# One-token attention block on one core: groups of one kv head over all batches instead of single (batch, head) pairs

## The chip, the core and the metric

The kernel runs on one core of a Trainium2 chip. A core has a matrix engine (TensorE, PE in the profile, with its weight loads as PEld), VectorE (DVE), ScalarE (ACT), GpSimd (POOL) and SyncE (SP), and 16 transfer engines (DMA) that move data between the device memory and the on-chip buffer (SBUF). TensorE writes its results to eight accumulation banks (PSUM, 128 partitions of 512 fp32 each), which VectorE and ScalarE read. Each engine works through its own list of instructions in order; the lists are tied together by semaphores, on which an instruction waits until another engine or a transfer has counted them up.

The metric is device time in microseconds. The kernel before takes 202.87 us (median of three runs, 202.81 to 203.03).

## The reference

Everything is bf16 in and out. Four batches, one token each, D = 512, 32 query heads, 8 kv heads, head size 128; of a cache of 16384 positions only the last W = 4096 are used.

```python
x  = A_x                                   # 4 x 1 x 512
xn = layernorm(x)
q  = (xn @ wq) per head                    # wq 512 x 4096, 4 MB
k  = k_cache[:, :, Sk - 4096:, :]          # 4 x 8 x 4096 x 128, 32 MB of the cache
v  = v_cache[:, :, Sk - 4096:, :]          # the same, 32 MB
p  = softmax(q k^T * 128**-0.5)            # 4 query heads share one kv head
A  = concat(p v) @ wo                      # wo 4096 x 512, 4 MB
B  = (silu(xn @ w_gate) * (xn @ w_up)) @ w_down   # 512 x 1792, 512 x 1792, 1792 x 512
out = x + A + B
```

In all 81 MB are read for very little arithmetic: each K and V row is used by four query heads of one batch only.

## The kernel before, in words

**Units and buffers.** The work is cut into 32 pairs, each one batch and one kv head. A pair's K is 1 MB and is loaded as a tile of 128 partitions, 32 rows of 128 numbers (8 KB) in each partition (`kv_ap`, L135); V likewise. There are four K buffers and four V buffers (`NSL`). All loads go through SP's queue (L159 to L192) in the order W_Q in two halves, x, K of pair 0, W_gate, W_up, W_down, V of pair 0, then K and V of each further pair, and W_O in eight parts of 512 KB. `load_k` (L161) waits until the pair four before has been transposed, `load_v` (L166) until the PV product that last read its buffer is done.

**Start.** GpSimd makes the identity and some selection matrices (L140 to L157). VectorE and ScalarE make the layer norm; TensorE transposes it, makes q for all heads (L295), the gate and up products (L303) and, once the gated product `guT` is there, the W_down product (L311).

**One pair.** TensorE runs a hardware loop of 8 turns, four pairs in each (L363 to L369). For a pair it runs two "spin" matmuls of 512 columns whose result nobody reads (L333), 32 transpositions of K tiles into four PSUM banks, eight in each (L321), the PV product of the pair before (L336 to L344: one matmul that sums the probabilities, then 32 matmuls with a V tile as the stationary operand and 4 columns moving), one more spin, and 32 score matmuls with a transposed K tile as the stationary operand and the 4 query columns moving (L327). VectorE copies each bank of eight transposed tiles to SBUF (L239). The scores of a pair are 128 x 128 numbers in one bank; ScalarE takes their Exp in one instruction, without subtracting a maximum (L202). VectorE then sums, inverts and normalises (`norm`, L241 to L249).

**End.** The normalised heads are rearranged by selection matmuls (L349), multiplied with W_O in four column tiles of the array (L357; a column tile is a strip of 32 columns that holds its own small stationary operand and writes its own 32 PSUM partitions), added up in one bank with x and the W_down product, cast by VectorE (L279) and written out by four small transfers, two from SP and two from ScalarE.

The order of all this is written out by hand; no planner moves anything.

```python
for r in Fori(8):            # L363
    for b in range(4):
        spin(2); transposes(r, b); pv(r, b); spin(1); scores(r, b)
```

Of the kernel before, what the change touches and what calls it, by code (L numbers as in the profile page):

```python
# [10 lines left out]
def bass_parallel_sum__sliding_block_cached__swiglu_ffn__decode_kernel(  # L11
# [18 lines left out]
    NT = W // 128  # L30
# [3 lines left out]
    NPAIR = B * HKV  # L34
    NSL = 4
    NG = 4
    SCALE = float(Dh) ** -0.5
    EPS = 1e-5

    sb = nc.alloc_sbuf_tensor  # L40
    X = sb("x_sb", [B, D], BF16)
# [9 lines left out]
    WQ = sb("wq_sb", [128, NC, HQ * Dh], BF16)  # L51
    WG = sb("wg_sb", [128, NC, F], BF16)
    WU = sb("wu_sb", [128, NC, F], BF16)
    WD = sb("wd_sb", [128, NF, D], BF16)
    WO = sb("wo_sb", [128, HKV, REP, D], BF16)
    QT = sb("qT", [128, HKV, B, REP], BF16)
    QC = sb("qC", [128, B, REP], BF16)
    KB = [sb("kbuf%d" % s, [128, NT, Dh], BF16) for s in range(NSL)]
    VB = [sb("vbuf%d" % s, [128, NT, Dh], BF16) for s in range(NSL)]
    KT = [sb("kT%d" % s, [128, NT, 128], BF16) for s in range(2)]  # L60
    P = [sb("p%d" % s, [128, NT, REP], BF16) for s in range(2)]
    den = sb("den", [128, REP], FP32)
    OT = sb("oT", [128, HKV, REP, B], BF16)
    OP = sb("oP", [128, REP, HKV, B], BF16)
    ex = sb("ex", [128, NF, B], FP32)
    gs = sb("gs", [128, NF, B], FP32)
    guT = sb("guT", [128, NF, B], BF16)
    ident = sb("ident", [128, 128], BF16)
    sel = sb("sel", [128, REP, REP, 32], BF16)
    ones = sb("ones", [128, 128], BF16)  # L70
    I4 = sb("i4", [B, B], FP32)
    y0 = sb("y0", [B, D], FP32)
    I4w = sb("i4w", [B, 32], FP32)
    y = sb("y_sb", [128, 128], BF16)

    ps = nc.alloc_psum_tensor
    ps_kt = [ps("ps_kt%d" % s, [128, 512], FP32) for s in range(4)]
    ps_S = ps("ps_s", [128, 512], FP32)
    ps_O = ps("ps_o", [128, 512], FP32)
    ps_m = ps("ps_m", [128, 512], FP32)  # L80
    ps_acc = ps("ps_acc", [128, 512], FP32)

    kt_ps = [t[:].bitcast(BF16).rearrange("p (a b) -> p a b", b=128) for t in ps_kt]
    O_ps = ps_O[:, 0:REP]
    den_ps = ps_O[:, 128:128 + NT * REP]
    gate_ps = ps_m[:, 0:NF * B]
    up_ps = ps_m[:, 64:64 + NF * B]
    perm_ps = ps_m[:].rearrange("p (e k h b) -> p h e k b", e=REP, k=HKV, h=REP)
    q_ps = ps_acc[:, 0:HQ * B]
    down_ps = ps_acc[0:B, :]  # L90
    xT_ps = ps_m[:, 128:128 + NC * B]

    def sem(name):
        return nc.alloc_semaphore(name=name)
    d_x = sem("d_x")
    d_wq = [sem("d_wq%d" % h) for h in range(2)]
    d_wg = sem("d_wg")
    d_wu = sem("d_wu")
    d_wd = sem("d_wd")
    d_out = sem("d_out")  # L100
    d_wo = [sem("d_wo%d" % q) for q in range(HKV)]
    d_k = [sem("d_k%d" % s) for s in range(NSL)]
    d_v = [sem("d_v%d" % s) for s in range(NSL)]
    s_const = sem("s_const")
    s_var = sem("s_var")
# [4 lines left out]
    s_q = sem("s_q")  # L110
    s_gu = sem("s_gu")
    s_ex = sem("s_ex")
    s_guT = sem("s_guT")
    s_tr = sem("s_tr")
    s_ev = sem("s_ev")
    s_sc = sem("s_sc")
    s_p = sem("s_p")
    s_pv = sem("s_pv")
    s_nrm = sem("s_nrm")
    s_pm = sem("s_pm")  # L120
    s_pc = sem("s_pc")
    s_acc = sem("s_acc")
    s_dn = sem("s_dn")
    s_y0 = sem("s_y0")
# [3 lines left out]
    out_ap = out.rearrange("b s (n c) -> n (b s) c", n=NC)  # L128
    wq_ap = A_wq.rearrange("(p c) n -> p c n", c=NC)
# [3 lines left out]
    wo_ap = A_wo.rearrange("(k p e) n -> k p e n", k=HKV, e=REP)  # L133

    def kv_ap(cache, i):  # L135
        return cache[i % B, i // B, Sk - W:, :].rearrange("(p t) d -> p t d", t=NT)

    with nc.Block() as block:

        @block.gpsimd  # L140
        def _(eng):
            eng.memset(ident[:], 0.0)
            eng.memset(I4[:], 0.0)
            eng.memset(I4w[:], 0.0)
            eng.memset(ones[:], 1.0)
            eng.drain()
            eng.affine_select(I4[:], I4[:], pattern=[[-1, B]], compare_op=ALU.not_equal,
                              fill=1.0, base=0, channel_multiplier=1)
# [3 lines left out]
            eng.tensor_copy(I4w[:, 0:B], I4[:])  # L152
            for e in range(REP):
                for h in range(REP):
                    eng.tensor_copy(sel[:, e, h, :], ident[:].rearrange("p (m e) -> p e m", e=REP)[:, e, :])
            eng.memset(P[1][:], 0.0)
            eng.memset(VB[NSL - 1][:], 0.0).then_inc(s_const, 1)  # L157

        @block.sync  # L159
        def _(eng):  # L160
            def load_k(i):  # L161
                if i >= NSL:
                    eng.wait_ge(s_tr, NG * (i - NSL + 1))
                eng.dma_start(KB[i % NSL][:], kv_ap(A_k_cache, i)).then_inc(d_k[i % NSL], 16)  # L164

            def load_v(i):  # L166
                if i == NSL - 1:
                    eng.wait_ge(s_pv, 1)
                if i >= NSL:
                    eng.wait_ge(s_pv, i - NSL + 2)  # L170
                eng.dma_start(VB[i % NSL][:], kv_ap(A_v_cache, i)).then_inc(d_v[i % NSL], 16)  # L171

            def load_wo(q):
                eng.dma_start(WO[:, q], wo_ap[q]).then_inc(d_wo[q], 16)  # L174

            eng.dma_start(WQ[:, 0:2], wq_ap[:, 0:2]).then_inc(d_wq[0], 16)
            eng.dma_start(X[:], x_ap).then_inc(d_x, 16)
            eng.dma_start(WQ[:, 2:4], wq_ap[:, 2:4]).then_inc(d_wq[1], 16)
# [4 lines left out]
            load_v(0)  # L183
            for i in range(1, NPAIR):
                load_k(i)
                load_v(i)
            for q in range(HKV):
                load_wo(q)
            eng.wait_ge(s_y, 1)
            for n in range(0, NC, 2):  # L190
                eng.dma_start(out_ap[n], y[32 * n:32 * n + B, :]).then_inc(d_out, 16)
            eng.wait_ge(d_out, 16 * NC)  # L192

        @block.scalar
        def _(eng):
            eng.wait_ge(s_var, 1)
            eng.activation(st_std[:], st_var[:], ACT.Sqrt).then_inc(s_std, 1)
            eng.wait_ge(s_gu, 1)
            eng.activation(ex[:], gate_ps.rearrange("p (t b) -> p t b", b=B), ACT.Exp, scale=-1.0).then_inc(s_ex, 1)  # L199
            for j in range(NPAIR):  # L200
                eng.wait_ge(s_sc, j + 1)
                eng.activation(P[j % 2][:], ps_S[:, 0:NT * REP].rearrange("p (t h) -> p t h", h=REP),  # L202
                               ACT.Exp, scale=SCALE).then_inc(s_p, 1)
            eng.wait_ge(s_y, 1)
            for n in range(1, NC, 2):
                eng.dma_start(out_ap[n], y[32 * n:32 * n + B, :]).then_inc(d_out, 16)

        @block.vector
        def _(eng):
# [17 lines left out]
            eng.tensor_copy(XnT[:], xT_ps.rearrange("p (c b) -> p c b", b=B)).then_inc(s_xnT, 1)  # L227
            eng.wait_ge(s_q, 1)
            eng.tensor_copy(QT[:], q_ps.rearrange("p (k h b) -> p k b h", k=HKV, b=B))
            eng.drain()  # L230
            eng.tensor_copy(QC[:], QT[:, 0]).then_inc(s_nrm, 1)

            eng.engine_nop().then_inc(s_ev, 3)

            def evac(i):
                for g in range(NG * i, NG * i + NG):
                    eng.wait_ge(s_tr, g + 1)
                    a = 8 * (g % NG)
                    eng.tensor_copy(KT[i % 2][:, a:a + 8, :], kt_ps[g % 4]).then_inc(s_ev, 1)  # L239

            def norm(j):  # L241
                eng.wait_ge(s_pv, j + 2)
                if j + B < NPAIR:
                    eng.tensor_copy(QC[:, j % B], QT[:, j // B + 1, j % B])  # L244
                eng.tensor_reduce(den[:], den_ps.rearrange("p (t h) -> p h t", h=REP), AX.X, ALU.add)  # L245
                eng.drain()
                eng.reciprocal(den[:], den[:])  # L247
                eng.drain()
                eng.tensor_tensor(OT[:, j // B, :, j % B], O_ps, den[:], ALU.mult).then_inc(s_nrm, 1)  # L249

            def ffn():
                eng.wait_ge(s_ex, 1)
                eng.tensor_scalar(ex[:], ex[:], 1.0, None, ALU.add)  # L253
                eng.drain()
                eng.reciprocal(ex[:], ex[:])
                eng.drain()
                eng.tensor_tensor(gs[:], gate_ps.rearrange("p (t b) -> p t b", b=B), ex[:], ALU.mult)
                eng.drain()
                eng.tensor_tensor(guT[:], up_ps.rearrange("p (t b) -> p t b", b=B), gs[:], ALU.mult).then_inc(s_guT, 1)  # L259

            def perm_copy(n, a, b):
# [151 lines left out]
```

## Time and profile before

| what | value |
|---|---|
| median of three runs | 202.87 us |
| profiled execution, first to last instruction (span) | 201.0 us |
| profiled execution, its own time | not listed beside its span; the runs stand 1.8 to 2.0 us above it |
| TensorE busy | 167.7 us (83%) |
| TensorE weight loads busy | 142.7 us (71%) |
| VectorE busy | 108.7 us (54%) |
| ScalarE busy | 11.9 us (6%) |
| bytes read, mean rate over the span | 81.01 MB, 403 GB/s |
| mean granted TensorE clock | 0.934 of full |

How to read it. The page cuts the span into 40 slices of about 5 us and gives for each the busy tenths of every engine, the granted clock of TensorE (PEclk, in tenths of full speed), the share in which the 16 transfer engines were busy, and the rate in GB/s. A group row names a line of the kernel, an engine, an operation, output and input tiles with their shapes, how often it ran, its busy time in us with the mean duration of one in ns, and the idle time of the engine just before it with what ended most of that. A timeline row gives the start, the duration, the engine and line, and how many instructions are merged in it; matmuls overlap, so a row of 32 matmuls lasts less than 32 of their durations. In a chain row (start, duration, what) "issue" is time in which the engine waited for nothing that the profile shows. A window row gives a stretch, then busy time and count of PE, PEld, DVE, ACT and POOL, the granted clock, the busy share of the transfer engines and the rate.

### The profile page before, as it was taken

Reading aid. Unit: us, or ns where it says so; the run is one execution under the profiler, and the core shown is the slowest. Engines: PE = TensorE matmul, PEld = TensorE weight load, DVE = VectorE, ACT = ScalarE, POOL = GpSimd, SP = SyncE. Lnnn points to the kernel's source line nnn. Section 1 sums busy time; section 2 is a strip of 40 time slices with the busy share of each in tenths; the row PEclk is TensorE's granted clock in tenths of the full one; section 3 lists DMA queues with packets and bytes.
Section 4 is the critical chain, followed back from the end, with each engine's and each line's share of the span. In section 5 each row is a group of like instructions: output and inputs, shape, how many; then the busy total and the mean of one; then the engine's idle time right before and its main releaser. Section 6 shows DMA issues by size and latency. Waiting matters only on the chain.

```text
span 201.0 us, 8038 instructions
## 1 busy us (share of the span) xinstructions
PE 167.7 (83%) x3635; PEld 142.7 (71%) x3635; DVE 108.7 (54%) x277; ACT 11.9 (6%) x36; POOL 7.2 (4%) x29
## 2 busy tenths in 40 slices
PE   0043778999899999999999999988898999898982
PEld 0043662788798888788877987777777987796961
DVE  0330010666666777766666666666665676565740
ACT  2020000010000000001000000000000000000000
POOL 8600000000000000000000000000000000000000
PEclk9999999999969999999999799999998899878755
DMA  6999999999999999999999999999999999999980
GB/s 232 428 425 426 431 418 414 421 417 424 422 411 419 422 422 426 422 419 419 424 422 424 422 416 421 422 424 422 422 419 421 424 424 422 421 419 412 410 334 7
DMA packets 11138, 81.15 MB, mean 404 GB/s; under 512 B 1268, under 2 KB 1272, under 8 KB 2296
## 3 DMA queue, kind: packets, MB, share of 16 engines
q1 hardware_dynamic: 11112, 81.01, 97.2%
q8 instruction: 6, 0.10, 0.2%
q14 instruction: 4, 0.03, 0.0%
q10 hardware_dynamic: 16, 0.00, 0.0%
HBM read 81.01 MB, written 0.00 MB: 403 GB/s over the span
## 4 chain that ended last, share of the span: by engine, by line
DMA 52%; PE 27%; DVE 13%; SPq 5%; issue 2%; ACT 0%; DVEq 0%
DMA kbuf<-in_A_k_cache_dram 32%; DVE kT L239 12%; DMA wu_sb<-in_B_w_up_dram 11%; PE ps_kt L321 10%; DMA wo_sb<-in_A_wo_dram 9%; PE ps_s L327 6%; SPq L174 3%; PE ps_m L333 3%; PE ps_o L343 3%; PE ps_acc L311 3%; PE ps_m L303 2%; SPq L171 1%; PE ps_o L341 0%; PE ps_acc L357 0%; SPq L164 0%
## 5 line engine op out<-in xcount | busy, mean ns | idle before, releaser
L239 DVE COPY kT<-ps_kt 128x1024 bf16<-128x1024 bf16 x128 | 80.9, 684 | 51.9 <-PE ps_kt L321 51.8
L321 PEld LDWEIGHTS ps_kt<-ident,kbuf 128*128 128x128 bf16 x1024 | 65.3, 104 | 15.1 <-issue 7.9
L321 PE MATMUL ps_kt<-ident,kbuf 128*128 128x128 bf16 x1024 | 69.4, 231 | 4.3 <-DMA kbuf<-in_A_k_cache_dram 4.2
L327 PEld LDWEIGHTS ps_s<-qC,kT 128*128 128x128 bf16 x1024 | 28.2, 96 | 12.5 <-DVE kT L239 12.0
L327 PE MATMUL ps_s<-qC,kT 128*128 128x4 bf16 x1024 | 30.4, 164 | 4.2 <-DVE kT L239 4.2
L343 PE MATMUL ps_o<-p,vbuf 128*128 128x4 bf16 x1056 | 31.5, 165 | 0.0
L343 PEld LDWEIGHTS ps_o<-p,vbuf 128*128 128x128 bf16 x1056 | 30.4, 96 | 0.8 <-issue 0.8
L333 PE MATMUL ps_m<-wq_sb,ones 128*128 128x512 bf16 x96 | 31.0, 377 | 0.0
L202 ACT ACTIVATE p<-ps_s 128x128 bf16<-128x128 f32 x32 | 8.9, 277 | 152.5 <-PE ps_s L327 152.5
L287 PE MATMUL ps_m<-i,xn 4*128 4x4 f32 x4 | 0.6, 254 | 12.3 <-DVE xn L225 12.3
L245 DVE TENSOR_REDUCE den<-ps_o 128x4 f32<-128x128 f32 x32 | 9.0, 283 | 0.6 <-PE ps_o L343 0.4
L287 PEld LDWEIGHTS ps_m<-i,xn 4*128 4x128 f32 x4 | 0.6, 208 | 12.3 <-issue 12.3
L341 PE MATMUL ps_o<-p,ones 128*128 128x128 bf16 x33 | 7.5, 228 | 0.7 <-issue 0.7
L333 PEld LDWEIGHTS ps_m<-wq_sb,ones 128*128 128x128 bf16 x96 | 7.0, 96 | 0.4 <-issue 0.4
L303 PE MATMUL ps_m<-xnT,wg_sb 128*128 128x4 bf16 x56 | 3.5, 199 | 4.4 <-DMA wg_sb<-in_B_w_gate_dram 4.4
L247 DVE RECIPROCAL den<-den 128x4 f32<-128x4 f32 x32 | 5.7, 178 | 2.7 <-issue 0.4
L249 DVE TENSOR_TENSOR oT<-ps_o,den 128x4 bf16<-128x4 f32 x32 | 5.4, 168 | 2.7 <-issue 0.4
L253 DVE TENSOR_SCALAR ex<-ex 128x56 f32<-128x56 f32 x1 | 0.2, 192 | 12.0 <-ACT ex L199 12.0
L303 PEld LDWEIGHTS ps_m<-xnT,wg_sb 128*128 128x128 bf16 x56 | 3.4, 159 | 4.5 <-DMA wg_sb<-in_B_w_gate_dram 4.5
L311 PE MATMUL ps_acc<-wd_sb,guT 128*4 128x512 bf16 x14 | 5.1, 542 | 1.7 <-DVE guT L259 1.7
L357 PE MATMUL ps_acc<-wo_sb,oP 128*4 128x128 bf16 x128 | 4.3, 305 | 1.7 <-DMA wo_sb<-in_A_wo_dram 1.7
L244 DVE COPY qC<-qT 128x4 bf16<-128x4 bf16 x28 | 4.4, 158 | 1.2 <-PE ps_o L343 1.0
(46 smaller groups left out, 41.8 us busy)
## 6 DMA issues: line engine op xcount, KB each, us to landing
kbuf<-in_A_k_cache_dram SPq DMA_DIRECT2D x32, 1024.0 KB, 15.5
vbuf<-in_A_v_cache_dram SPq DMA_DIRECT2D x32, 1024.0 KB, 13.7
wq_sb<-in_A_wq_dram SPq DMA_DIRECT2D x2, 2048.0 KB, 9.4
wo_sb<-in_A_wo_dram SPq DMA_DIRECT2D x8, 512.0 KB, 18.4
wg_sb<-in_B_w_gate_dram SPq DMA_DIRECT2D x1, 1792.0 KB, 18.5
wu_sb<-in_B_w_up_dram SPq DMA_DIRECT2D x1, 1792.0 KB, 22.3
wd_sb<-in_B_w_down_dram SPq DMA_DIRECT2D x1, 1792.0 KB, 26.1
out_dram<-y_sb SPq DMA_DIRECT2D x2, 1.0 KB
```

The costliest lines, as they stand in the source:

```text
L174: eng.dma_start(WO[:, q], wo_ap[q]).then_inc(d_wo[q], 16)
L202: eng.activation(P[j % 2][:], ps_S[:, 0:NT * REP].rearrange("p (t h) -> p t h", h=REP), ACT.Exp, scale=SCALE).then_inc(s_p, 1)
L239: eng.tensor_copy(KT[i % 2][:, a:a + 8, :], kt_ps[g % 4]).then_inc(s_ev, 1)
L245: eng.tensor_reduce(den[:], den_ps.rearrange("p (t h) -> p h t", h=REP), AX.X, ALU.add)
L247: eng.reciprocal(den[:], den[:])
L303: last = mm(o[:, t * B:(t + 1) * B], w[:].rearrange("p c (m t) -> p c t m", t=NF)[:, c, t, :], XnT[:, c, :], start=(w is WG and t == 0 and ...
L311: last = mm(down_ps, guT[:, t, :], WD[:, t, :], start=(t == 0), stop=(t == NF - 1))
L321: last = eng.transpose(kt_ps[n % 4][:, k, :], KB[b][:, 8 * g + k, :], ident[:])
L327: last = mm(ps_S[:, REP * t:REP * (t + 1)], KT[b % 2][:, t, :], QC[:, b])
L333: mm(ps_m[:], ones[:], WQ[:, 0, 0:512])
L341: mm(den_ps, ones[:], P[p % 2][:].rearrange("p t h -> p (t h)"))
L343: last = mm(O_ps, VB[p][:, t, :], P[p % 2][:, t, :], start=(t == 0), stop=(t == NT - 1))
```

## The change

The unit becomes a group: one kv head of all four batches, 8 groups of 4 MB of K and 4 MB of V. A partition holds 128 rows of one batch (32 KB in one run), partition p belonging to batch p mod 4.

- *Buffers and queue.* Two K buffers and two V buffers of 4 MB. The second V buffer is W_Q's space (so V of group 1 waits for q), W_O later takes the first K buffer's (so W_O waits for the transpositions of group 6). SP's order: W_Q in one load, K0, W_gate, W_up, K1, V0, then K and V in turn, V7 in two halves, W_down, W_O in five parts of 16, 8, 5, 2 and 1 rows a partition. x comes by ScalarE's queue. K of group r waits for the last transposition of group r-2, V of group r for the PV product of group r-2.
- *Scores.* A group is 16 chunks of eight tiles, over two PSUM banks for the transpositions. TensorE issues the transpositions of chunk n+1, then the scores of chunk n, which wait for the copy of chunk n. VectorE copies three chunks of four, ScalarE every fourth. A score matmul has 16 moving columns, the 4 heads of all 4 batches. Four banks hold the scores of a group; into each a matmul first writes a mask of -1e30 wherever a partition's batch and a column's batch differ.
- *Maximum.* VectorE takes the maximum of each score bank; at the end of a group a TensorE transposition and a few VectorE operations make the negative maximum of each column, which four more matmuls of 512 columns add to the banks. Then ScalarE takes the Exp of each bank (four instructions of 512).
- *PV.* The probabilities of two tiles (32 columns) are the stationary operand, V of two tiles (256 columns) moves, and four column tiles take turns: 64 matmuls for a group, run one group later behind that group's scores. VectorE copies the result and sums; fp32 matmuls fold the parts together; VectorE divides.
- *End.* One transposition and 16 selection matmuls rearrange the heads; W_down and 24 of the 32 W_O rows go into four column tiles of one bank, are copied, folded by fp32 matmuls with the last 8 W_O rows added, and one transfer writes the output.
- All four engines' main work stands in hardware loops of 4 turns with two groups in each.

```diff
-            for i in range(1, NPAIR):
-                load_k(i)
-                load_v(i)
+            def load_k(r):
+                if r >= 2:
+                    eng.wait_ge(s_tr[r % 2][NCH - 1], r // 2)
+                eng.dma_start(KB[r % 2][:].rearrange("p t d -> p (t d)"), kv_ap(A_k_cache, r)).then_inc(d_k[r % 2], 16)
+            def load_v(r, half=None):
...
+                if r == 1:
+                    eng.wait_ge(s_q, 1)
+                if r >= 1 and half != 1:
+                    eng.wait_ge(s_pv[(r - 1) % 2], (r - 1) // 2 + 1)
...
+            eng.dma_start(WQ[:], wq_ap).then_inc(d_v[1], 16)
             load_k(0)
             eng.dma_start(WG[:], wg_ap).then_inc(d_wg, 16)
             eng.dma_start(WU[:], wu_ap).then_inc(d_wu, 16)
+            load_k(1)
+            load_v(0)
+            for r in range(2, HKV):
+                load_k(r)
+                load_v(r - 1)
+            load_v(HKV - 1, 0)
+            load_v(HKV - 1, 1)
             eng.dma_start(WD[:], wd_ap).then_inc(d_wd, 16)
+            for q, (a, b) in enumerate(ROWS):
+                if q == 0:
+                    eng.wait_ge(s_tr[0][NCH - 1], HKV // 2)
+                eng.dma_start(WO[:, a:b, :], wo_ap[:, a:b, :]).then_inc(d_wo[q], 16)
...
 (scalar)
+            with eng.Fori(0, HKV // 2) as i:
+                for g in range(2):
+                    for n in range(3, NCH, 4):
+                        eng.wait_ge(s_tr[g][n], i + 1)
+                        eng.copy(KT[n % 2][:], kt_ps[n % 2]).then_inc(s_ev[g][n], 1)
+                    for q in range(NB):
+                        eng.wait_ge(s_sh[g][q], i + 1)
+                        eng.activation(P[g][:, q * TB:(q + 1) * TB, :], S_ps[q], ACT.Exp,
+                                       scale=SCALE).then_inc(s_xp[g][q], 1)
...
 (vector)
+                    for n in range(NCH):
+                        if n % 4 != 3:
+                            evac(i, g, n)
+                        if n % 4 == 1 and n > 4:
+                            bank_max(i, g, n // 4 - 1)
+                    bank_max(i, g, NB - 1)
+                    eng.drain()
+                    for e in range(2):
+                        eng.tensor_reduce(mxd[:, 32 * e:32 * e + CQ], mxb[:].rearrange("p q c -> p c q"), AX.X, ALU.max)
...
+            def sums(sems, v):
+                s_v, s_o, s_l, s_n, slot = sems
+                eng.wait_ge(s_v, v)
+                eng.tensor_copy(o4[:], o4_ps)
+                eng.tensor_reduce(dpart[:], ps_den[:].rearrange("p (t c) -> p c t", c=CQ), AX.X, ALU.add)
+                eng.drain().then_inc(s_o, 1)
...
 (tensor)
+            def scores(i, g, n):
+                q = n // 4
+                if n % 4 == 0:
+                    eng.wait_ge(s_xp[1 - g][q], i + 1)
+                    mm(S_ps[q], Lsel[:], bc(Dmask[:], TB), start=True, stop=False, skip_group_check=True)
+                eng.wait_ge(s_ev[g][n], i + 1)
+                for k in range(8):
+                    last = mm(S_ps[q][:, 8 * (n % 4) + k, :], KT[n % 2][:, k, :],
+                              QT[:, bass.ds(2 * i + g, 1), :, :].rearrange("p o b h -> p (o b h)"),
+                              start=False, stop=False, skip_group_check=True)
+            def pv(e, a, b):
+                for u in range(a, b):
+                    k = u % 4
+                    last = mm(o4_ps[32 * k:32 * k + 32, :], P[e][:, 2 * u:2 * u + 2, :].rearrange("p t c -> p (t c)"),
+                              VB[e][:, 2 * u:2 * u + 2, :].rearrange("p t d -> p (t d)"),
+                              start=(u < 4), stop=(u >= NT // 2 - 4), skip_group_check=True)
+            eng.wait_ge(s_qc, 1)
+            eng.wait_ge(s_guT, 1)
+            with eng.Fori(0, HKV // 2) as i:
+                for g in range(2):
+                    spin(4)
+                    transposes(i, g, 0)
+                    for n in range(NCH):
+                        if n + 1 < NCH:
+                            transposes(i, g, n + 1)
+                        scores(i, g, n)
+                    eng.wait_ge(d_v[1 - g], 16 * i + 16)
+                    for q in range(NB):
+                        eng.wait_ge(s_xp[1 - g][q], i + 1)
+                    den(1 - g)
+                    eng.wait_ge(s_nm[1 - g], i + 1)
+                    pv(1 - g, 0, 24)
+                    eng.wait_ge(s_cm[g], i + 1)
+                    eng.transpose(mx_ps, mxd[:], identf[:]).then_inc(s_mt[g], 1)
+                    pv(1 - g, 24, 64).then_inc(s_pv[g], 1)
+                    eng.wait_ge(s_dd[g], i + 1)
+                    for q in range(NB):
+                        mm(S_ps[q], Lsel[:], bc(Dsh[:], TB), start=False, stop=True,
+                           skip_group_check=True).then_inc(s_sh[g][q], 1)
+                    sums(s_oc[g], s_sl[g], i + 1)
```

More of the change, by code (lines that the diff above doesn't have):

```diff
@@ L86, in bass_parallel_sum__sliding_block_cached__swiglu_ffn__decode_kernel @@
[L86 to L91, printed above, removed]
+    S_ps = [t[:].rearrange("p (t c) -> p t c", c=CQ) for t in ps_S]
+    mx_ps = ps_kt[0][:, 0:128]
+    o4_ps = ps_O[:, 0:256]
+    dn_ps = ps_O[:, 256:256 + CQ]
+    ot_ps = ps_O[:, 288:288 + CQ]
+    xT_ps = ps_S[0][:, 0:NC * B]
+    q_ps = ps_S[1][:, 0:HQ * B]
@@ L230, in _ @@
+            eng.wait_ge(s_ex, 1)
+            eng.tensor_scalar(ex[:], ex[:], 1.0, None, ALU.add)
             eng.drain()
[L231 to L245, printed above, removed]
[L246 to L249 removed]
@@ L251, in ffn @@
[L251 to L261, printed above, removed]
-                eng.wait_ge(s_pm, n)
-                for h in range(REP):
-                    last = eng.tensor_copy(OP[32 * h:32 * h + 32, :, a:b], perm_ps[32 * h:32 * h + 32, h, :, a:b])
-                last.then_inc(s_pc, 1)
@@ L307, in _, with spin, transposes @@
             last.then_inc(s_gu, 1)
-            eng.wait_ge(s_guT, 1)
+            def spin(n):
+                for _ in range(n):
+                    mm(ps_den[:], ones[:], sel2[:, 0].rearrange("k q p -> k (q p)"))
+            def transposes(i, g, n):
+                if n == 0:
+                    eng.wait_ge(d_k[g], 16 * i + 16)
+                for k in range(8):
+                    last = eng.transpose(kt_ps[n % 2][:, k, :], KB[g][:, 8 * n + k, :], ident[:])
+                last.then_inc(s_tr[g][n], 1)
@@ new lines, in _ @@
+            last = HKV // 2
+            for q in range(NB):
+                eng.wait_ge(s_xp[1][q], last + 1)
+            eng.wait_ge(d_v[1], 16 * (last + 1))
+            den(1)
+            eng.wait_ge(s_nm[1], last + 1)
+            pv(1, 0, 32)
+            eng.wait_ge(d_vb, 16)
+            pv(1, 32, 64).then_inc(s_pv[0], 1)
+            mm(part_ps[0:32, :], I4w[:], X[:], start=True, stop=False, skip_group_check=True)
+            sums(s_oc[0], s_sl[0], last + 1)
+            eng.wait_ge(s_nm[0], last + 1)
@@ L309, in _ @@
+            eng.transpose(rt_ps, OT[:, 1:, :].rearrange("p r c -> p (r c)"), ident[:]).then_inc(s_rt, 1)
+            eng.wait_ge(s_rn, 1)
+            for b in range(B):
+                for q in range(4):
+                    m = mm(op_ps[:, b, :], sel2[:, b, q, :], Rn[:, 32 * q:32 * q + 32],
+                           start=(b == 0 and q == 0), stop=(q == 3), skip_group_check=True)
+            m.then_inc(s_op, 1)
             eng.wait_ge(d_wd, 16)
             for t in range(NF):
-                last = mm(down_ps, guT[:, t, :], WD[:, t, :], start=(t == 0), stop=(t == NF - 1))
@@ L362, in _ @@
-            eng.wait_ge(s_nrm, 1)
-            with eng.Fori(0, HKV) as r:
-                for b in range(B):
-                    spin(2)
-                    transposes(r, b)
-                    pv(r, b)
-                    spin(1)
-                    scores(r, b)
-            eng.wait_ge(s_y0, 1)
-            permute(0, HKV - 1)
+                k = (t + 1) % 4
+                mm(part_ps[32 * k:32 * k + 32, :], guT[:, t, :], WD[:, t, :], start=(t < 3), stop=False,
+                   skip_group_check=True)
```

356 lines of the change are left out of this document (206 added, 150 removed).

## The prediction

> **What bounds the kernel now.** I read the page first: its busy line, the slices of transfer rate and granted clock, then the windows by stage, the chain of waits, the timeline of one steady pair.
>
> ```profile
> span 201.0 us, 8038 instructions
> ...
> PE 167.7 (83%) x3635; PEld 142.7 (71%) x3635; DVE 108.7 (54%) x277; ACT 11.9 (6%) x36; POOL 7.2 (4%) x29
> ...
> PEclk9999999999969999999999799999998899878755
> ...
> GB/s 232 428 425 426 431 418 414 421 417 424 422 411 419 422 422 426 422 419 419 424 422 424 422 416 421 422 424 422 422 419 421 424 424 422 421 419 412 410 334 7
> ...
> 10.00:25.00 15.00, 7.70 (x188) 7.48 (x188) 2.32 (x8) 1.49 (x2) 0.00 (x0) 1.00 1.00 427
> 60.00:170.00 110.00, 103.56 (x2316) 88.87 (x2314) 72.14 (x185) 6.38 (x23) 0.00 (x0) 0.97 1.01 422
> ```
>
> The last two rows are windows; their last two columns are the busy share of the 16 transfer engines and GB/s. From slice 2 to slice 38 the transfers never pause: the kernel moves its 81 MB at 422 GB/s and ends some 3 us behind the last byte. The compute keeps up with little in reserve. One pair (1 MB of K, 1 MB of V) in the steady stage:
>
> ```profile
> 40.18 0.59 PE L333 MATMUL ps_m<-wq_sb,ones 128*128 128x512 bf16 x2
> ...
> 40.61 1.95 PE L321 MATMUL ps_kt<-ident,kbuf 128*128 128x128 bf16 x32
> 41.26 2.48 DVE L239 COPY kT<-ps_kt 128x1024 bf16<-128x1024 bf16 x4 [1.36 <-PE ps_kt L321]
> ...
> 43.80 0.95 PE L327 MATMUL ps_s<-qC,kT 128*128 128x4 bf16 x32 [0.16 <-DVE kT L239]
> ...
> 44.62 0.59 PE L333 MATMUL ps_m<-wq_sb,ones 128*128 128x512 bf16 x2
> ```
>
> Spin to spin is 44.62 - 40.18 = 4.44 us, against 2.1 MB / 422 GB/s = 4.97 us of transfer. Four pairs: 17.8 us of compute against 19.9. So transfers pace it, by 2 us in 20.
>
> The same rows give the prices of the new loop. A transposition: (1.95 - 0.22) / 31 = 56 ns from start to start. Eight of them until their copy can start: 41.26 - 40.61 = 0.65 us. From the end of the copies (43.74) to the first score 0.06; a score (0.95 - 0.16) / 31 = 25 ns. A 512-column matmul: about 0.216 (0.59 less a last one of 0.377). For the other engines:
>
> ```profile
> L239 DVE COPY kT<-ps_kt 128x1024 bf16<-128x1024 bf16 x128 | 80.9, 684 | 51.9 <-PE ps_kt L321 51.8
> ...
> L333 PE MATMUL ps_m<-wq_sb,ones 128*128 128x512 bf16 x96 | 31.0, 377 | 0.0
> ...
> L245 DVE TENSOR_REDUCE den<-ps_o 128x4 f32<-128x128 f32 x32 | 9.0, 283 | 0.6 <-PE ps_o L343 0.4
> L202 ACT ACTIVATE p<-ps_s 128x128 bf16<-128x128 f32 x32 | 8.9, 277 | 152.5 <-PE ps_s L327 152.5
> ...
> L357 PE MATMUL ps_acc<-wo_sb,oP 128*4 128x128 bf16 x128 | 4.3, 305 | 1.7 <-DMA wo_sb<-in_A_wo_dram 1.7
> ...
> L157 POOL MEMSET vbuf<- 128x4096 bf16 x1 | 3.5, 3517 | 0.0
> ...
> L155 POOL COPY sel<-ident 128x32 bf16<-128x32 bf16 x16 | 2.4, 200 | 0.0
> ...
> L211 DVE TENSOR_REDUCE st_sum<-x_sb 4x1 f32<-4x512 bf16 x1 | 0.7, 675 | 8.0 <-DMA x_sb<-in_A_x_dram 8.0
> ...
> L287 PE MATMUL ps_m<-i,xn 4*128 4x4 f32 x4 | 0.6, 254 | 12.3 <-DVE xn L225 12.3
> ...
> L229 DVE CAST qT<-ps_acc 128x128 bf16<-128x128 f32 x1 | 0.3, 293 | 3.7 <-PE ps_acc L295 3.7
> ...
> L199 ACT ACTIVATE ex<-ps_m 128x56 f32<-128x56 f32 x1 | 0.2, 217 | 16.3 <-PE ps_m L303 16.3
> ```
>
> ScalarE: 60 ns for 72 columns, 0.83 ns each on 0.17 us, so a copy of 1024 takes 1.02 us and an Exp of 512 takes 0.60. A VectorE reduction of 512 is 0.68, a copy of 256 fp32 about 0.43.
>
> **The change, part by part.**
>
> *Longer runs.* K and V, 67.1 MB, come in 32 KB runs instead of 8 KB. The window 10 to 25 us holds 14 and 16 KB runs (W_Q, gate, up) at 427 GB/s against 422: read as a fixed cost per run, that goes to about 430 at 32 KB, 159.0 to 156.1 us. Worth 2.9 us if transfers still set the pace; bounds 0 (no further gain) and 4. By the Trainium skill ("DMA: Bandwidth & Descriptors", Bandwidth) 435 GB/s is the ceiling of the path, which would make it 4.7 us; no slice here exceeds 431.
>
> *Start.* Ahead of W_up, K now has 4.2 MB where it had 1.05, and the loop waits for gate and up, their sums living in a score bank.
>
> ```profile
> 3.11 22.34 DMA wu_sb<-in_B_w_up_dram
> 25.45 0.05 issue
> 25.50 3.54 PE ps_m L303 x56
> ...
> 30.44 0.23 DVE guT L259
> ```
>
> W_up lands 3.15 MB / 427 GB/s = 7.4 us later, at 32.9; from landing to the gated product 25.50 to 30.67, 5.2 us, is unchanged. The loop starts at 38.0 (before at 35.7, since W_down's 5 us go to the end). X on ScalarE's queue, one wait for all 4 MB of W_Q, and POOL's longer list of masks (some 10 us, at the memset's 0.86 ns a column and about 0.2 for each small operation, in place of 2.4 + 3.5 and some small ones) cost nothing: q is wanted only at 38. VectorE's q copy, now queued behind POOL's last mask, has 20 us of cover; were it gone, a late POOL would count in full.
>
> *The chunk loop*, per group 16 chunks of 8 tiles with two transposition banks. TensorE issues T(n+1), S(n); S(n) waits for copy n, and T(n+2) is queued behind S(n). Round trip for two chunks: copy 0.685, to the scores 0.06, eight scores 0.20, to the next copy 0.65, in all 1.59. Before, four banks let four copies run in a row (2.48 / 4 = 0.62 each). Every fourth copy is ScalarE's: +0.33. VectorE's bank maximum (0.68) stands between copies 5 and 6 of a block and delays the sixth by some 0.6, of which about 0.25 remains on the path. Four chunks: 3.18 + 0.33 + 0.25 = 3.76; a group 15.0 us. The mask matmul (0.216, four per group) runs while TensorE waits for a copy. TensorE itself needs 11.4 of the 15.0. Sixteen columns per score instead of four: at 25 ns the column count is not the limit; taken as free. The q slice is now addressed by a register, which has no row; the dearest small matmul here (L303, 3.54 / 56 = 63 ns) bounds that at +38 ns a score, 0.30 in each round trip and 2.4 us a group.
>
> *The seam*, from the last score to the next group's first transposition: bank maximum 0.16 + 0.68, two reductions and drains 0.55, together 1.4, beside which the sums of P and 24 of the PV matmuls run (1.0). Then the fp32 transposition, 0.45 (nearest row L287, 0.25 for one of four columns), and 40 PV matmuls 1.2 (VectorE's minimum and the two operations on it, 0.9, go beside them). Then 0.2 until VectorE sees PV, copy 0.43, reduction 0.68, drain 0.1; the four shift matmuls (0.86) are hidden under these. Then three fp32 matmuls 0.6 (0.25 each alone, partly overlapped) and four spins 0.86. Sum 5.9. ScalarE's four Exps (2.4) are done before the next group's fourth chunk, the first that queues behind them.
>
> PV in four column tiles: 64 matmuls of 256 columns replace 128 of 4. Nearest row, W_O's four column tiles of 128 columns:
>
> ```profile
> 193.00 1.88 PE L357 MATMUL ps_acc<-wo_sb,oP 128*4 128x128 bf16 x64
> ```
>
> 25 ns each, where one alone streams 53 at full clock: at least two side by side. 256 columns are 107 ns; four together give 27 ns each (1.7 us a group), two together 53 (3.4). I take 29, since the burst of 16 in 0.60 us at 197.79 (19 ns each, quoted below) is nearer four. The Trainium skill ("TensorEngine Tiling (Array Packing)", Restrictions) says that column tiles lose the fast weight load and that changing the tiling mode drains the array. By that rule a group would carry four drains more, near 0.2 us by the latency of one matmul above (estimate), 0.8 us a group and 6 on the total; no row here separates it.
>
> A group is therefore 15.0 + 5.9 = 20.9 us, more than the 19.6 of its transfers at 428 GB/s: TensorE's chain becomes the bound.
>
> *The SP queue.* K of group r+2 waits for the last transposition of group r, with V(r+1)'s load queued behind it; V(r+1) waits for PV of group r-1. Before, SP also waited, but over 1 MB slots while data was still queued:
>
> ```profile
> SPq L171 <- PE ps_o L343: 134.1, 29, 24.3
> ```
>
> Now V0 has gone out at 2.4 + 20.4 MB / 427 = 50.2, and K2 may start only when group 0 is transposed, 38.0 + 0.9 + 14.5 = 53.4, plus 1.6 from issue to first bytes: the engines stand idle some 5 us there, and some 1.3 us in each later group (20.9 - 19.6). W_down, W_O and V7 are left for the end: V7 goes out near 38.0 + 7 x 20.9 - 2.4 + 1.6 = 183.5, then 10.2 MB, 23.9 us, W_O's last row landing near 209.
>
> *The tail.* Before:
>
> ```profile
> 190.53 0.42 PE L373 MATMUL ps_acc<-y,i4w 4*32 4x128 f32 x8
> ...
> 197.79 0.60 PE L357 MATMUL ps_acc<-wo_sb,oP 128*4 128x128 bf16 x16 [0.74 <-DMA wo_sb<-in_A_wo_dram]
> 198.44 0.29 DVE L279 CAST y_sb<-ps_acc 128x128 bf16<-128x128 f32 x1 [4.61 <-PE ps_acc L357]
> 198.76 0.63 SPq L191 DMA_DIRECT2D out_dram<-y_sb  x2
> ```
>
> After, behind the last group: sums and PV of group 7 2.1, to VectorE 0.2, copy and reduction 1.2, fp32 matmuls 0.6, reciprocal and product 0.4, transposition and copy 0.5, 16 selecting matmuls and their copy 0.9, 14 of W_down and 24 of W_O in column tiles 38 / 4 x 0.216 = 2.1, copy out 0.7, fold 0.4 (L373), 32 last matmuls 0.8, cast 0.3, output 2.2 (198.76 to 201.0 before). Sum 12.4.
>
> **Sum.** 38.0 + 8 x 20.9 + 12.4 = 217.6 us of span. The median of the runs, 202.87, stands 1.87 above the profiled span of 201.0 (no time of the profiled execution itself is listed); the same around the new span gives 219.5. W_O's landing at 209 plus some 3 us stays under it.
>
> **The rivals.**
>
> *Transfers still pace it (the other side).* If the chunk loop comes out shorter (round trip hidden, the bank maximum free: 12.7 us) with a short seam, a group takes 18.6 us or less, and this decides: 38.0 + 8 x 18.6 + 12.4 = 199.2. The longer runs then give 2.9 us, one output transfer in place of four perhaps 0.3, and the gap ahead of K2, 1.5 to 3 us, takes half or more of it back: span 198.5 to 200.5, time 200.4 to 202.4. For it: all rows of the loop are separate prices, TensorE's own work is 16 us a group. Against it: two banks, and a seam that nothing fills.
>
> *The clock falls.* The page's clock row drops when TensorE waits, and then:
>
> ```profile
> 154.34 3.44 PE L321 MATMUL ps_kt<-ident,kbuf 128*128 128x128 bf16 x32 [0.43 <-DMA kbuf<-in_A_k_cache_dram]
> ```
>
> 107 ns each instead of 56. If the gaps in the chunk loop did that throughout, eight transpositions to their copy take 1.05 (round trip 2.0) and spin, PV and shift double: some 26.8 us a group, 267 of span. Against it: the new loop's waits are under 0.6 us each, and the columns streamed (1024 + 128 of 2260 clocks in a chunk of 0.94 us, plus as many 512-column matmuls per megabyte as before) are as dense as in the window that had 0.97. A quarter of such a loss is in my range.
>
> *Aliased reads.* Each run of a batch lies 32 MB from the next. The Trainium skill ("DMA: Bandwidth & Descriptors", Latency and other measured facts) measured about half the rate for rows 4 or 8 MiB apart. At half of the 422 above, K and V would take 318 us and the kernel about 360. Against it: at any moment the engines would read neighbouring 32 KB runs of one batch, much as W_Q's at 427.
>
> **How the numbers follow.** TensorE's chain paces it, warm: 0.73, with group times from 18.9 to 22.4 us and so times of 203.5 to 232. Transfers pace it: 0.17. Clock lost: 0.08. Aliased reads: 0.02. A measurement of this kernel tells about 0.2% from no change, 202.5 to 203.3: that strip, where the first two cases meet, gets 0.03. So faster 0.16, same 0.03, slower 0.81. The range of 200.5 to 232 leaves out the last two cases and a few parts in a hundred at each end.
>
> **What would show it.** Right: transfer slices that dip below 400 in the middle, first at 50 to 55 us; the loop's first spin near 38; VectorE's copies 0.9 us apart on average in a group, their idle time ended by the transpositions; ScalarE's copy near 1.0 us; a seam of 5 to 6 us in each group; more than 10 us between the last group's seam and the end. Wrong: slices at 428 or more throughout with TensorE waiting for K, or copies 0.8 us apart; a ScalarE copy nearer 0.7 or bank maxima that fall into idle time would take 1 to 2 us off each group, eight times.

## The result, and the profile after

The changed kernel takes 220.69 us (median of four runs, 219.62 to 220.84) against 202.88 us for the kernel before: 1.0866 times as long, 95% interval 1.0843 to 1.089. The profiled execution took 220.78 us, 1.8 us more than its span.

The page of the kernel after; the slices are now 5.5 us each:

```profile
span 219.0 us, 6860 instructions
...
PE 165.5 (76%) x3150; PEld 129.0 (59%) x3158; DVE 115.2 (53%) x225; ACT 52.5 (24%) x69; POOL 10.8 (5%) x32
...
PEclk9999999999999999999999999999999999999979
...
GB/s 288 383 479 383 428 438 470 389 473 18 311 450 404 398 392 443 449 323 437 425 437 323 449 407 461 317 449 425 401 335 473 401 293 144 431 443 419 405 29 1
...
q1 hardware_dynamic: 3764, 81.01, 88.1%
...
PE 47%; DVE 22%; DMA 14%; ACT 8%; issue 3%; DVEq 3%; SPq 1%; ACTq 0%
```

The same two rows of the page before were:

```profile
q1 hardware_dynamic: 11112, 81.01, 97.2%
...
DMA 52%; PE 27%; DVE 13%; SPq 5%; issue 2%; ACT 0%; DVEq 0%
```

Before, the transfers ran without a pause and made up 52% of the chain. Now there is a hole (18 GB/s, the slice from 49 to 55 us), dips to between 317 and 335 in four later slices, four apart, a deep one (144) near 184 us, and a chain of TensorE, VectorE and ScalarE work. The granted clock in the page's row is full nearly throughout, so it is no slow TensorE that costs the time. The transfers themselves became cheaper: 88.1% of 219.0 us is 192.9 us of work for the 16 engines, against 97.2% of 201.0, 195.4 us, before.

Where the transfers wait is in the SP queue's own waits (engine and line, what it waited for, us in all, times, longest):

```profile
SPq L230 <- PE ps_kt L408: 128.6, 6, 50.2
...
SPq L240 <- PE ps_o L432: 18.9, 5, 3.8
```

L230 loads K and waits for the last transposition of two groups before; L240 loads V. Long waits alone say little, since much is queued ahead. That the queue ran dry is seen in the rate.

One group of the new loop, in the chain of waits (start, duration, what). First the group's spins, then a block of four chunks, then the seam. In the output names kT is the copy of transposed tiles in SBUF, ps_kt the transpositions (L462 is the fp32 one), ps_s the scores, mxb the bank maxima, ps_o the PV product and its fold, ps_den the spins; DVEq L337 is VectorE's drain behind its reduction of the sums of P:

```profile
60.92 0.81 PE ps_den L402 x3
...
64.55 1.02 ACT kT L277
65.57 0.05 issue
65.62 0.36 PE ps_s L418 x8
65.98 0.48 PE ps_kt L408 x8
66.45 0.02 issue
66.48 0.69 DVE kT L326
67.17 0.60 DVE mxb L330
67.77 0.61 DVE kT L326
...
76.22 0.37 PE ps_s L418 x8
76.61 0.69 DVE mxb L330
...
77.89 0.33 PE ps_kt L462
78.22 1.24 PE ps_o L432 x40
79.48 0.42 DVE o L335
79.90 0.64 DVEq L337
80.54 0.04 issue
80.58 0.40 PE ps_o L439 x2
80.98 0.45 PE ps_o L441 x4
81.43 0.06 issue
81.49 0.81 PE ps_den L402 x3
82.30 0.46 PE ps_kt L408 x8
```

The group begins with its spins at 60.92 (60.92 and 81.49 are two rows of the same line, L402; the trace lists three of the four spins) and is over at 81.49: 20.57 us. Nothing in it is a transfer.

### The profile page after: what moved, and what is told of

Read it like the earlier page. It is cut to its first block, busy times and chain, and to the rows that moved or that the text cites. A ratio compares the mean times of both kernels' runs of the same rounds, so it can differ in the third digit from the quotient of the medians.

```text
span 219.0 us, 6860 instructions
## 1 busy us (share of the span) xinstructions
PE 165.5 (76%) x3150; PEld 129.0 (59%) x3158; DVE 115.2 (53%) x225; ACT 52.5 (24%) x69; POOL 10.8 (5%) x32
## 3 DMA queue, kind: packets, MB, share of 16 engines
q1 hardware_dynamic: 3764, 81.01, 88.1%
## 4 chain that ended last, share of the span: by engine, by line
PE 47%; DVE 22%; DMA 14%; ACT 8%; issue 3%; DVEq 3%; SPq 1%; ACTq 0%
PE ps_kt L408 18%; DMA wu_sb<-in_B_w_up_dram 14%; DVE kT L326 12%; PE ps_s L418 11%; ACT kT L277 7%; DVE mxb L330 7%; PE ps_o L432 5%; PE ps_den L402 3%; DVEq L337 2%; PE ps_o L441 2%; PE ps_s L394 2%; DVE o L335 2%; PE ps_o L439 1%; PE ps_kt L462 1%; PE ps_s L415 1%
## 5 line engine op out<-in xcount | busy, mean ns | idle before, releaser
L326 DVE COPY kT<-ps_kt 128x1024 bf16<-128x1024 bf16 x96 | 65.4, 688 | 36.6 <-PE ps_kt L408 36.0
L418 PE MATMUL ps_s<-qT,kT 128*128 x1024 | 45.7, 171 | 15.8 <-DVE kT L326 10.5
L418 PEld LDWEIGHTS ps_s<-qT,kT 128*128 128x128 bf16 x1024 | 35.1, 96 | 32.9 <-DVE kT L326 18.3
L277 ACT COPY kT<-ps_kt 128x1024 bf16<-128x1024 bf16 x32 | 32.4, 1012 | 91.0 <-PE ps_kt L408 91.0
L330 DVE TENSOR_REDUCE mxb<-ps_s 128x16 f32<-128x512 f32 x32 | 21.9, 683 | 9.5 <-PE ps_s L418 9.5
L280 ACT ACTIVATE p<-ps_s 128x512 bf16<-128x512 f32 x32 | 16.5, 603 | 29.0 <-PE ps_s L466 29.0
L415 PE MATMUL ps_s<-dmask,lsel 128*128 128x512 bf16 x32 | 12.4, 387 | 0.0
L432 PE MATMUL ps_o<-wq_sb,p 128*32 128x256 bf16 x320 | 10.3, 273 | 0.0
L402 PE MATMUL ps_den<-sel,ones 128*128 128x512 bf16 x24 | 7.1, 409 | 3.0 <-DVE guT L319 2.5
L432 PE MATMUL ps_o<-vbuf,p 128*32 128x256 bf16 x256 | 8.5, 273 | 0.0
L466 PE MATMUL ps_s<-dsh,lsel 128*128 128x512 bf16 x32 | 8.3, 381 | 0.0
```

The source lines that it names most:

```text
L277: eng.copy(KT[n % 2][:], kt_ps[n % 2]).then_inc(s_ev[g][n], 1)
L280: eng.activation(P[g][:, q * TB:(q + 1) * TB, :], S_ps[q], ACT.Exp, scale=SCALE).then_inc(s_xp[g][q], 1)
L326: eng.tensor_copy(KT[n % 2][:], kt_ps[n % 2]).then_inc(s_ev[g][n], 1)
L330: eng.tensor_reduce(mxb[:, q, :], S_ps[q].rearrange("p t c -> p c t"), AX.X, ALU.max)
L402: mm(ps_den[:], ones[:], sel2[:, 0].rearrange("k q p -> k (q p)"))
L415: mm(S_ps[q], Lsel[:], bc(Dmask[:], TB), start=True, stop=False, skip_group_check=True)
```

## The experiments

Theory A: TensorE's chain (transposition, copy, score, and the seam at each group's end) sets the group time, and the transfers wait for it. Its rivals: the 4 MB transfers with their gaps hold the kernel back (B); the spins carry the clock (C); the later start is absorbed (D); the maximum lies beside other work (E). Edits are against the kernel after unless another is named.

**Half the bytes, the same waits.**

```diff
-                eng.dma_start(KB[r % 2][:].rearrange("p t d -> p (t d)"), kv_ap(A_k_cache, r)).then_inc(d_k[r % 2], 16)
+                m = (HALF if r >= 2 else NT) * Dh
+                eng.dma_start(KB[r % 2][:].rearrange("p t d -> p (t d)")[:, 0:m], kv_ap(A_k_cache, r)[:, :, 0:m]).then_inc(d_k[r % 2], 16)
```

> From group 2 on, only the first half of each partition's K and V run is loaded (the other half of the buffer keeps an older group's rows), so 25 MB less are moved in all and 4.2 instead of 8.4 MB per group; every wait and every matmul stays. Theory A (TensorE's chain of transposition, copy, score and seam sets the group time of 20.57 us): group time and total unchanged, 220 to 221 us, with transfer slices that fall to about half. Rival B (the 4 MB transfers with their idle gaps set the group time): a group falls below 17 us and the total below 195 us.

Measured: 219.76 us (219.05 to 220.47). Its page:

```profile
GB/s 272 404 464 401 415 454 446 419 440 60 290 478 389 33 359 380 12 57 413 302 0 145 428 199 0 250 392 130 0 347 347 78 0 97 422 422 440 405 99 1
```

and its spins, two groups in a row:

```profile
80.95 0.81 PE L404 MATMUL ps_den<-sel,ones 128*128 128x512 bf16 x3
101.52 0.81 PE L404 MATMUL ps_den<-sel,ones 128*128 128x512 bf16 x3
```

V's load is cut in the same way. Eleven loads were halved, 23 MB (V7's were left whole). The transfer engines now stand idle for whole slices and the group still takes 20.57 us. The median is 0.9 us lower, and the two runs lie about as the four of the kernel after do. Rival B is out: in the kernel after, the transfers of the loop cost nothing that a faster transfer would give back.

**No spins.** `spin(4)` at the head of a group is left out.

> The four spin matmuls at the head of each group are left out (their result is never read). Theory A: they lie on the chain at 0.81 us a group, so 7 groups give back 5.7 us and the first one about nothing (it starts at half clock with or without them): 214 to 216 us, granted clock still above 0.95. Rival C (the spins hold the clock): the clock drops below 0.9 in the chunk loops and the total rises to 228 us or more.

Measured: 214.86 us (214.11 to 215.62), 5.8 less. The sum came out, its parts did not. The first group, which was to give about nothing, gave 1.6 us: its first mask matmul stands at 40.06 instead of 41.70. The later groups take 19.77 and 20.23 us in turn (first mask matmuls at 60.48, 80.25 and 100.48), which is 0.57 less than 20.57 on average and not 0.81, since without the spins the next copy waits for VectorE's reciprocal and product. The blocks stay at 3.53 us (mask matmuls at 64.36, 67.90, 71.43) and the granted clock of the profiled execution is 1.0, so the clock holds without the spins: rival C is out for this loop.

**Gate and up ahead of K0.**

```diff
-            load_k(0)
             eng.dma_start(WG[:], wg_ap).then_inc(d_wg, 16)
             eng.dma_start(WU[:], wu_ap).then_inc(d_wu, 16)
+            load_k(0)
```

> W_gate and W_up are queued ahead of the first K load instead of behind it. Theory A: W_up lands near 23 us, the gated product is there near 28, and the first transposition waits only for K0, which lands near 32.7 instead of starting at 40.2; some of the first transpositions run at half clock, so 6 to 7.5 us less: 213 to 215 us. Rival D (the start is absorbed later, since the last loads or the tail end at the same time): 219 us or more.

Measured: 213.58 us (213.39 to 213.76), 7.1 less. Its timeline:

```profile
22.83 3.52 PE L394 MATMUL ps_s<-xnT,wu_sb 128*128 128x4 bf16 x56 [1.97 <-DMA wu_sb<-in_B_w_up_dram]
32.62 1.89 PE L408 MATMUL ps_kt<-ident,kbuf 128*128 128x128 bf16 x16 [2.23 <-DMA kbuf<-in_A_k_cache_dram]
```

The first transposition stands at 32.62 instead of 39.99 in the same view of the kernel after, and nearly all of that reaches the end. Rival D is out.

**No maximum.** As in the kernel before, no maximum is subtracted: bank maxima, reductions, the fp32 transposition and the shift matmuls go, and ScalarE's Exp waits for the scores.

```diff
-                        if n % 4 == 1 and n > 4:
-                            bank_max(i, g, n // 4 - 1)
-                    bank_max(i, g, NB - 1)
...
-                        eng.wait_ge(s_sh[g][q], i + 1)
+                        eng.wait_ge(s_sc[g][q], i + 1)
```

> The maximum is left out, as in the kernel before: no bank maxima, no reductions, no fp32 transposition, no shift matmuls; ScalarE takes the Exp of a bank as soon as its scores are done. Theory A: the loop loses about 1.2 us a group (VectorE's maxima delay the copies) and the seam about 0.9 (PV runs straight behind the scores, then copy, sums, spins), 18.5 us a group, under the 19.5 of its transfers, so that these with the gap ahead of K2 set the end: 202 to 205 us. Rival E (the maximum lies beside other work): 218 us or more.

Measured: 216.38 us (216.13 to 216.62), 4.3 less where 16 to 19 were expected: a miss. The group came down only to 19.81 us (spins at 59.88 and 79.69), by what the seam lost; the loop did not get shorter. ScalarE's copies in its timeline:

```profile
67.05 1.01 ACT L277 COPY kT<-ps_kt 128x1024 bf16<-128x1024 bf16 x1 [1.47 <-PE ps_kt L394]
...
70.58 1.01 ACT L277 COPY kT<-ps_kt 128x1024 bf16<-128x1024 bf16 x1 [1.47 <-PE ps_kt L394]
```

They stand 3.53 us apart, as in the kernel after (68.09 and 71.62 there). So a block of four chunks is set by the two round trips of which one goes through ScalarE's copy of 1.01, and VectorE's maximum had been hidden beside it. (The chain of the kernel after does run through the maximum, at 67.17: there the way through the maximum and the way through ScalarE's copy end within 0.1 us of each other, and a chain shows only one of the two.) Rival E is right for the loop and wrong for the seam. Theory A holds, but its division of the block fell; the new form (A1) was tried in the next two runs. Another 1.6 us of the gain were lost at the end: the last group's 64 PV matmuls took 3.56 us instead of 1.93, in a slice whose clock is 6 tenths.

**All copies on VectorE**, with the maximum and without it:

```diff
-                        if n % 4 != 3:
-                            evac(i, g, n)
+                        evac(i, g, n)
```

> All 16 copies of a group on VectorE, none on ScalarE; the bank maxima stay on VectorE. Theory A1 (a block of four chunks, 3.53 us, is set by ScalarE's copy of 1.02 us, and the bank maximum hides behind it): the block falls towards VectorE's own work, 4 x 0.65 + 0.68 = 3.3, 0.6 to 1.3 us a group less: 210 to 216 us. Theory A2, the prediction's terms (0.33 for ScalarE's copy, 0.25 for the maximum, each on the path): VectorE now has both, the block stays at 3.5 or rises to 3.7: 219 to 222 us.

Measured: 216.05 us (215.87 to 216.24), 4.6 less. VectorE's timeline in a block:

```profile
66.68 1.28 DVE L323 COPY kT<-ps_kt 128x1024 bf16<-128x1024 bf16 x2
68.28 1.34 DVE L323 COPY kT<-ps_kt 128x1024 bf16<-128x1024 bf16 x2 [0.32 <-PE ps_kt L404]
69.53 0.68 DVE L327 TENSOR_REDUCE mxb<-ps_s 128x16 f32<-128x512 f32 x1
70.13 1.28 DVE L323 COPY kT<-ps_kt 128x1024 bf16<-128x1024 bf16 x2
```

A block takes 70.13 - 66.68 = 3.45 us, four copies and a maximum with 0.3 us to spare: with the maximum, VectorE is nearly full and taking ScalarE's copy away is worth only 0.08 us a block once the loop runs evenly (the first and the last block of a group gave the rest of its 0.62 us).

> The maximum left out and all copies on VectorE. Theory A1: a block comes down to the two round trips, 3.18 us, a group to 19.8 - 4 x 0.35 = 18.4, below the time of its transfers, so that transfers and the gap ahead of K2 share the end: 202 to 206 us. Theory A2: leaving out the maximum gave nothing in the loop, so neither does this: 215 us or more.

Measured: 205.58 us (205.38 to 205.77), 10.8 less than without the maximum alone. The mask matmuls of three blocks in a row:

```profile
102.41 0.38 PE L397 MATMUL ps_s<-dmask,lsel 128*128 128x512 bf16 x1
...
105.62 0.38 PE L397 MATMUL ps_s<-dmask,lsel 128*128 128x512 bf16 x1
...
108.84 0.38 PE L397 MATMUL ps_s<-dmask,lsel 128*128 128x512 bf16 x1
```

Blocks of 3.21 us, the two round trips and no more; groups of 18.52. Transfers did not share the end, as A1 had it: they are 15% of this kernel's chain, all of it the wait for W_up at the start, so TensorE's chain still sets the time. Either edit alone gave 4 to 5 us, both together 15: each engine hid the other's delay. In numbers, a steady block takes 3.53 with ScalarE's copy alone, 3.45 with the maximum alone, 3.53 with both and 3.21 with neither.

**The seam opened, everything together.** On top of the last kernel and the early gate, the fp32 matmuls that fold PV's parts go behind the fourth chunk of the next group, so that TensorE does not wait at the seam for VectorE's copy and reduction:

```diff
                         scores(i, g, n)
+                        if n == 3:
+                            sums(s_oc[1 - g], s_sl[g], i + 1)
...
-                    sums(s_oc[g], s_sl[g], i + 1)
```

> Together: gate and up first, no maximum, all copies on VectorE, and the fp32 matmuls that fold PV's parts (with reciprocal and product) moved behind the fourth chunk of the next group, so that the seam is only the sums of P, 64 PV matmuls and the spins. A group needs some 16 us of TensorE's chain, and K2 can go out before V0 is through. Theory A (the long runs do help once TensorE's chain is out of the way): transfers run without a gap, 81.0 MB / 430 GB/s from 2.4 us on, some 2 us to the last landing and 3 to the end, span 195 to 197, 197 to 199 us, below the kernel before. Rival B (the 4 MB loads themselves hold the kernel back): 202 us or more.

Measured: 198.50 us (198.08 to 198.77), 0.9774 of the kernel before, 95% interval 0.9758 to 0.979. It beats both kernels. Its page:

```profile
GB/s 214 446 418 432 453 443 433 433 430 426 403 418 423 440 430 433 426 426 433 433 426 426 426 426 433 426 426 440 433 433 433 440 426 423 413 424 427 425 367 30
```

A group of the chain takes 17.7 to 17.9 us (PV starts at 85.06, 102.73 and 120.58), the transfers of one 19.5 at 430 GB/s, and there is no hole left: the kernel is bound by its transfers again. Like the kernel before, and unlike the kernel after, it subtracts no maximum.

**Short runs in that kernel.** The 4 MB of a group's K or V go out as four loads of 1 MB with 8 KB runs.

> As e6_late_sums, but each 4 MB of K and V goes out as four loads of 1 MB with 8 KB runs, as in the kernel before. If the run length is worth what the prediction took (430 against 422 GB/s over 67.1 MB): 2.9 us slower than e6_late_sums. If it is worth nothing: within 0.5 us of it.

Measured: 202.26 us (ten runs, 201.76 to 202.84), 3.76 more, about where the kernel before stands (0.9964 of it, interval 0.9953 to 0.9975). The windows from 60 to 170 us, long runs first, then short (the last column is GB/s):

```profile
60.00:170.00 110.00, 101.56 (x2077) 83.60 (x2077) 74.70 (x124) 14.93 (x25) 0.00 (x0) 1.00 1.00 431
```

```profile
60.00:170.00 110.00, 99.17 (x2026) 81.37 (x2024) 72.34 (x119) 14.34 (x24) 0.00 (x0) 1.00 1.01 420
```

So 32 KB runs in 4 MB loads are worth 11 GB/s over 8 KB runs in 1 MB loads here, in a kernel that can use them. Run length and number of loads changed together in this run; which of the two it is stays open.

## Why the prediction was right

The time came out at 220.69 where 219.5 was predicted, and for the reason given: TensorE's chain, at 20.57 us a group, sets the time, and the transfers wait for it. That the total came so close is in part luck, since terms that were too large and too small cancel. Step by step:

- *The start.* The loop was to begin at 38.0. W_up's matmuls began at 32.65, the gated product was there at 38.0, the first spin on record ran at 38.72. Right. That the first spins and transpositions run at half clock was left out: 1.48 us for three spins instead of 0.81 (the durations show it; the clock row reads full there).
- *The chunk loop*, 15.0 us. Measured 14.95, from the first transposition (61.56) to the first matmul behind the last scores (76.51). The total is right partly by luck. The first scores of the four blocks and that last matmul:

```profile
63.05 0.35 PE L418 MATMUL ps_s<-qT,kT 128*128 x8 [0.22 <-DVE kT L326]
...
66.49 0.35 PE L418 MATMUL ps_s<-qT,kT 128*128 x8
...
70.03 0.36 PE L418 MATMUL ps_s<-qT,kT 128*128 x8
...
73.56 0.36 PE L418 MATMUL ps_s<-qT,kT 128*128 x8
...
76.51 0.40 PE L426 MATMUL ps_den<-p,ones 128*32 128x512 bf16 x4
```

  Until the first scores 1.49 us pass, which the sum had left out; the blocks then take 3.44, 3.54, 3.53 and 2.95 (the last has no next transpositions behind it), where the sum had 3.76 four times. The two delays that it added to the round trips' 3.18 were each sized well: ScalarE's copy alone makes a block 3.53 - 3.21 = 0.32 longer (0.33 was taken), the maximum alone 3.45 - 3.21 = 0.24 (0.25 was taken). What failed is adding them. They lie beside each other, and both together cost 0.32, the larger of the two.
- *Sixteen columns and an address from a register.* Eight scores take 0.36, so (0.36 - 0.17) / 7 = 27 ns from start to start; taken as free, and free.
- *The seam*, 5.9 us. From 76.51 to 82.14, 5.6, and in the predicted order: maximum, transposition, 40 PV matmuls, copy and reduction, fold, spins.
- *PV in column tiles*, 29 ns each. 40 in 1.24 us, with (1.24 - 0.27) / 39 = 25 ns: all four side by side. The drain that the Trainium skill ("TensorEngine Tiling (Array Packing)", Key Properties) attaches to a change of tiling mode does not show at the prediction's estimate of 0.2 us when the column tiles begin. At the first seam the last eight scores start at 55.64 and follow at 27 ns, the last of them at 55.83; the first column tile starts at 55.93. So this switch costs less than 0.1 us. The switch back stands beside other waits and was not priced.
- *The group*, 20.9 us: 20.57 for each but the first, which takes 22.20 (spins at 38.72 and 60.92), its first spins and transpositions running at half clock. Over seven groups the differences nearly cancel: 7 x 20.9 = 146.3 against 145.6 (38.72 to 184.36).
- *The SP queue.* K2 was to go out at 53.4 and went at 54.57; V7 near 182 (183.5 with the way to its first bytes), and it went at 182.34. The hole and the smaller dips are where they were said to be.
- *The tail*, 12.4 us. Measured from the last fold (205.34, rows of the timeline) to the end, 13.7. Two things were too small: TensorE waits 0.7 us for ScalarE's last Exps, and W_down and W_O began at half clock (the granted clock is 0.50 from 211.5 to 213.3 us): 38 matmuls took 3.4 us instead of 2.1. The waits of 0.84, 0.60 and 0.32 us ahead of them do not explain that alone: in the profiled execution of the run with half the bytes the same waits stand there, the clock stays at 1.0, and the 38 matmuls take 2.3 us. Why it fell stays open.

```profile
205.54 0.40 PE L426 MATMUL ps_den<-p,ones 128*32 128x512 bf16 x4 [0.68 <-ACT p L280]
...
211.43 1.89 PE L491 MATMUL ps_s<-wd_sb,guT 128*32 128x512 bf16 x14
```

- *Longer runs*, 2.9 us if transfers set the pace: 3.76 where they did, 431 GB/s against 420. The direction was right, the size too small; the window that it was priced from also holds the 1 MB of K of pair 0, in 8 KB runs. That a fixed cost per run is the cause is not shown, as said above. In the kernel after they are worth nothing, as predicted: there even half the bytes gave nothing in the group time. With these runs single slices swing (479 beside 383 in the kernel after), so the mean of 431 over 110 us is what counts; it stays under the 435 that the prediction names.
- *The rivals.* Transfers pacing the kernel was the other side, from 18.6 us a group downwards. That point was put too high, or needs the early start: with 18.52 us groups TensorE's chain still set the time (205.6), and only with 17.7 to 17.9 and the early start did the transfers (198.5). The rival's own price, 200.4 to 202.4, did not hold at 18.52; the hole ahead of K2 remained there (106 GB/s in that run's worst slice). The clock did not fall in the loop. Aliased reads did not occur: the same 32 KB runs of four batches came at 431 GB/s in the kernel with the seam opened.

Two more things are only argued: what two transposition banks cost instead of four (more were not tried, all eight PSUM banks being in use), and what the opened seam gives by itself, since it was run only together with the other edits.

## What to carry to other kernels

Cut the loop into round trips (who waits for whom, in the order of the in-order queue) and price each from rows of the kernel that is there; a change that improves the resource which paces a kernel is worth nothing when it lengthens the chain next in line beyond it, and here that one had 2 us in 20 to give. When two engines take turns in such a trip, taking away either one's delay alone gives little and both together much, so price them as a maximum, not as a sum. And fold results of one unit behind the first steps of the next: the seam cost more than a quarter of each group, and opening it, with the rest, turned a loss of 8.7% into a gain of 2.3%.

## What was not expected

The bank maximum on VectorE cost nothing in a steady block beside ScalarE's 1.01 us copy. TensorE kept its full clock in the chunk loop without a single spin (mean clock 1.0 in that profiled execution). In the tail the clock row of the kernel after drops to 7 tenths behind waits of 0.84, 0.60 and 0.32 us, and with the same waits it does not drop in the run with half the bytes. And 23 MB less to load, more than a quarter of all bytes, changed the time by 0.9 us.
